# A two-layer decode step on one core: the ninth half rows of the second up projection move to the upper partitions and to GpSimd's queue

## The chip, the core and the metric

The kernel runs on one core of a Trainium2 chip. A core has TensorE (PE), VectorE (DVE), ScalarE (ACT), GpSimd (POOL) and SyncE (SP), an on-chip memory of 128 partitions, and 16 DMA engines that bring data from HBM. Each compute engine follows its own instruction list in order; SP's list holds almost nothing but transfers. The metric is the device time of one execution in microseconds (us), as the median of several.

## The reference

Two layers, each a cached attention and a gated MLP, for two sequences and one new token each; the same weights and the same caches serve both layers. All data are float32.

```python
def attn(x, k_cache, v_cache, wq, wo):      # x: [2, 1, 576]; caches: [2, 32, 8192, 128]
    q = (x @ wq).reshape(2, 1, 32, 128).transpose(0, 2, 1, 3)
    p = softmax(einsum("bhqd,bhkd->bhqk", q, k_cache) * 128 ** -0.5)
    o = einsum("bhqk,bhkd->bhqd", p, v_cache)
    return o.transpose(0, 2, 1, 3).reshape(2, 1, 4096) @ wo
def mlp(x, w_gate, w_up, w_down):           # 576 -> 4608 -> 576
    return (gelu(x @ w_gate) * (x @ w_up)) @ w_down

for _ in range(2):
    x = x + attn(layernorm(x), ...)
    x = x + mlp(layernorm(x), ...)
```

## The kernel before, in words

All large data go through one tile, `space` (L133), of 50176 floats in each of the 128 partitions. A small planner, `Arena` (L68), places every transfer in it. The transfers are written down in one order by `plan_first`, `plan_mlp(0)`, `plan_second` and `plan_mlp(1)` (L324 to L418), and `pump` (L148) issues them from SP in that order as soon as the next one has a place. A place is given back by `done` (L152), after the instructions that read it. `fit` (L107) places the weights of the second layer: first just behind the last one placed, then from the start of `space`, then behind each live region, whichever is clear.

Attention works through 34 items, each two heads (or one) of one sequence. DVE multiplies keys by the query (L644), POOL folds the products (L661), DVE sums them (L664), ACT takes the exponentials (L721), and PE multiplies by the values (L762). In the second layer the items come in reverse. Then `project` (L807) multiplies by eight groups of output weights (L812), in the order 7 to 0, and `add_to_x` (L520) adds the result to x.

`mlp(1)` is where the change lies. `norm` (L486) writes the centred x, transposed, into `xt`: in the window of 32 columns that belongs to u = 0..8, partition p holds the element of x that goes with weight row (9p + u) / 2, in the first or in the second pair of columns by whether 9p + u is even or odd. Its last step is POOL's power (L517). The weights lie in half rows: a row of `w_up` (4608 floats) is cut into two, and of the 1152 half rows partition p holds those with numbers 9p to 9p + 8 (`half_rows`, L221). The gate weights come in three transfers of three half rows per partition. The up weights come in two of three (u = 0..2 and 3..5) and three of one (u = 6, 7, 8), by `GU` (L305). A half row has 2304 floats, 9 KB.

`all_products` (L959) takes them in this order: for each u, two column halves v and four column groups c, a product at L967 of an 8-column window of `xt` with 288 weight columns, added up in `acc`. `activate` (L973) then forms gelu(gate) times up, on ACT and DVE, for the two column halves. Last come the down weights, in eight transfers (`DOWN[1]`, L311) of 9, 9, 5, 4, 3, 3, 2 and 1 rows of 576 floats per partition, and their products at L1004. Between the down products stand a few products without a result (`idle_products`, L524). `add_to_x` and two small output transfers (L1019) end the kernel.

POOL has no work between L517 and the end, and issues no transfer anywhere in the kernel. ACT issues eight small loads of x at the start (L140), two rows each, and one of the two output transfers.

Of the kernel before, what the change touches and what calls it, by code (L numbers as in the profile page):

```python
# [9 lines left out]
F32 = mybir.dt.float32  # L10
# [5 lines left out]
P = 128  # L16
B = 2
# [8 lines left out]
HALF = P // 2  # L26

GH = 4
NU = 9
EQ = 512  # L30
HG = DF // 16
PAD = 6
# [90 lines left out]
def decode_layers(ctx, tc, x_in, kc, vc, wq, wo, wg, wu, wd, out):  # L123
    nc = tc.nc
    scale = DH ** -0.5

    consts = ctx.enter_context(tc.tile_pool(name="consts", bufs=1))
# [15 lines left out]


    arena = Arena()
    queue, ready, places = [], {}, {}

    def pump():  # L148
        while queue and queue[0]():
            queue.pop(0)  # L150

    def done(key):  # L152
        arena.free(key)
        pump()

    def part_at(at, n):
        return space[:, at:at + n]
# [51 lines left out]
    def weights(key, n, first, transfers):  # L209

        def make():
            at = arena.ring(key, n) if first is None else arena.fit(key, n, first)
            if at is None:
                return False
            t = ready[key] = part_at(at, n)
            transfers(t)
            return True

        queue.append(make)

    def half_rows(key, w, us, first):  # L221

        width = w.shape[1] // 2
        rows = w.rearrange("r (s w) -> (r s) w", w=width).rearrange("(p u) w -> p u w", p=P)

        def transfers(t):
            nc.sync.dma_start(t.rearrange("p (u w) -> p u w", w=width), rows[:, us[0]:us[-1] + 1, :])

        weights(key, len(us) * width, first, transfers)

    def of_half(h, k):

        width = wq.shape[1] // 2
        rows = wq.rearrange("r (s w) -> (r s) w", w=width).rearrange("(p u) w -> p u w", p=P)

        def transfers(t):
            for e in range(2):
                nc.sync.dma_start(t[e::2, :], rows[e::2, 2 * k + (h + e) % 2, :])

        weights(("wq", 1, h, k), width, None, transfers)  # L240

    def split_rows(name, w, h, u):

        rows = w[:, DF // 2 * h:DF // 2 * (h + 1)].rearrange("(m r) w -> m r w", r=NU)

        def transfers(t):
            for e in range(2):
                nc.sync.dma_start(t[e::2, :], rows[:, 5 * e + u, :])

        weights((name, 0, h, u), DF // 2, None, transfers)  # L250

    def split_middle(h):

        def transfers(t):
            for g, w in enumerate((wg, wu)):
                for e in range(2):
                    lo, n = DF // 4 * (2 * h + e), DF // 4
                    nc.sync.dma_start(
                        t[e::2, n * g:n * (g + 1)], w[:, lo:lo + n].rearrange("(m r) w -> m r w", r=NU)[:, 4, :]
                    )  # L260

        weights(("gu", 0, h), DF // 2, None, transfers)
# [136 lines left out]
    def plan_mlp(layer):  # L399
        if layer == 0:  # L400
            for h in range(2):
                for u in range(4):
                    split_rows("g", wg, h, u)
                split_middle(h)
                for u in range(4):
                    split_rows("u", wu, h, u)
        else:
            for g, (name, w) in enumerate((("g", wg), ("u", wu))):
                for us in GU[g]:
                    half_rows((name, layer, us[0]), w, us, 0)  # L410
        for rows in DOWN[layer]:
            down(layer, rows)

    plan_first()
    plan_mlp(0)
    plan_second()
    plan_mlp(1)
    pump()  # L418


    ident = consts.tile([P, P], F32, name="ident")
# [37 lines left out]

    xt = consts.tile([P, PAD + NU * 32], F32, name="xt")
    nc.vector.memset(xt, 0.0)


    acc = psum1.tile([P, 2, 512], F32, name="acc")
# [13 lines left out]
    def small(p, n):  # L480

        smalls.append(smalls.pop(0))
        return smalls[0][0:p, 0:n]
# [36 lines left out]
    def add_to_x():  # L520
        nc.vector.tensor_add(x, xps, x)  # L521
# [409 lines left out]
    def mlp(layer):  # L931
        split = layer == 0
        rstd = norm(split)
        if split:
            idle_products(3)
        hT = once.tile([P, 2, NI, 2, 2, B], F32, name="hT", tag="xc")

        def window(u, at):

            return xt[:, PAD + 32 * u - at:PAD + 32 * u - at + 4 * B]  # L940

        def split_products(h):

            steps = [(("g", layer, h, u), u, 2, (0,)) for u in range(4)] + [(("gu", layer, h), 4, 1, (0, 1))]
            steps += [(("u", layer, h, u), u, 2, (1,)) for u in range(4)]
            for key, u, sides, gs in steps:
                w = ready.pop(key).rearrange("p (k c w) -> p k c w", c=4, w=HG)
                for k in range(2):
                    g, e = (k, 0) if u == 4 else (gs[0], k)
                    for c in range(4):  # L950
                        nc.tensor.matmul(
                            acc[32 * c:32 * c + 4 * B, h, :HG], window(u, 4 * g + 2 * e), w[:, k, c, :],
                            start=(key == steps[0][0] and k == 0), stop=(key == steps[-1][0] and k == 1),
                        )
                done(key)
                if key != steps[-1][0]:
                    idle_products(1)

        def all_products():  # L959

            for g, name in enumerate("gu"):
                for us in GU[g]:
                    w = ready.pop((name, layer, us[0])).rearrange("p (u v c w) -> p u v c w", v=2, c=4, w=HG)
                    for u in us:
                        for v in range(2):
                            for c in range(4):
                                nc.tensor.matmul(  # L967
                                    acc[32 * c:32 * c + 4 * B, v, :HG], window(u, 4 * g), w[:, u - us[0], v, c, :],
                                    start=(g == 0 and u == 0), stop=(g == 1 and u == NU - 1),
                                )  # L970
                    done((name, layer, us[0]))

        def activate(v):  # L973

            o = once.tile([P, 2, HG], F32, name="o", tag="row")
            nc.scalar.activation(o[:, 0, :], acc[:, v, :HG], AF.Copy, scale=rstd)  # L976
            gu = o[:, 1, :].rearrange("p (i r) -> p i r", i=NI)
            nc.vector.transpose(gu, o[:, 0, :].rearrange("p (m i) -> p i m", i=NI))  # L978
            g = gu[:, :, 0:4]
            a = once.tile([P, NI, 4], F32, name="ga", tag="part")  # L980
            nc.vector.tensor_mul(a, g, g)
            nc.vector.tensor_scalar(a, a, 0.044715, 1.0, op0=ALU.mult, op1=ALU.add)
            nc.vector.tensor_mul(a, a, g)
            nc.scalar.activation(a, a, AF.Tanh, scale=math.sqrt(2.0 / math.pi))
            nc.vector.scalar_tensor_tensor(a, a, 1.0, g, op0=ALU.add, op1=ALU.mult)
            nc.vector.tensor_mul(a, a, gu[:, :, 4:8])
            a, to = a.rearrange("p i (e b) -> p (i e) b", b=B), hT[:, v].rearrange("p i e s b -> p (i e) s b")
            nc.vector.tensor_scalar_mul(to[:, :, 0, :], a, 0.5)
            nc.scalar.mul(to[:, :, 1, :], a, 0.5)

        if not split:
            all_products()
        for v in range(2):
            if split:
                split_products(v)
            activate(v)
        for n, rows in enumerate(DOWN[layer]):
            if n < len(IDLE[layer]):
                idle_products(IDLE[layer][n])
            w = ready.pop(("d", layer, rows[0])).rearrange("p (i c) -> p i c", c=D)  # L1000
            for k, (t, i) in enumerate(rows):
                v, e = divmod(t, 2) if split else (t % 2, t // 2)
                for c in range(4):
                    nc.tensor.matmul(  # L1004
                        xps[32 * c:32 * c + 2 * B, :], hT[:, v, i, e, :, :].rearrange("p s b -> p (s b)"),
                        w[:, k, c * CW:(c + 1) * CW],
                        start=(rows is DOWN[layer][0] and k == 0), stop=(t, i) == (NT - 1, NI - 1),
                    )
            done(("d", layer, rows[0]))
        add_to_x()  # L1010
        if layer == 0:
            idle_products(1)

    attention(0)
    mlp(0)
    attention(1)
    mlp(1)
# [29 lines left out]
```

## Time and profile before

| | |
|---|---|
| median of 3 runs | 2686.62 us (2686.51 to 2686.68) |
| profiled execution, first to last instruction (its span) | 2685.0 us |
| DMA queue q1 (SP), share of 16 engines' span | 99.8%, 1153.19 MB |
| DVE, POOL, PE busy | 67%, 43%, 34% |
| ACT busy | 6% |
| mean DMA rate | 430 GB/s |

The profiled execution has no other time of its own than its span; the runs' times include some 1.6 us around it. The page gives busy times per engine, the span in 40 slices with the share of the 16 DMA engines that was in use, and the chain of work that ended last. In a group's row stand line, engine, operation, what it writes and reads, count, busy time in us and mean in ns, and after a bar the idle time ahead of it with what ended most of it. In a timeline row the start and the duration come first, in us from the start of the span. In a row of time windows stand the window, its length, busy time and count for PE, weight loads, DVE, ACT and POOL, and then the granted PE clock, the share of the DMA engines in use, and GB/s. No view numbers the DMA engines.

### The profile page before, as it was taken

How to read it: one execution, taken by the hardware profiler on the slowest of the kernel's cores; microseconds unless marked ns; L12 is line 12 of the kernel's file. 1: busy time of each engine (PE TensorE's matmuls, PEld its weight loads, DVE VectorE, ACT ScalarE, POOL GpSimd, SP SyncE). 2: the span in 40 equal slices, each digit the busy share in tenths (PEclk: the TensorE clock that was granted, in tenths of full speed). 3: DMA queues.
4: the chain of work that ended last, by engine and by line, in shares of the span. 5: the costliest groups of instructions: out<-in, count | busy, mean ns of one | idle time of the engine just before them, and what ended most of it. 6: DMA issues, size and time to landing. Idle time of an engine off the chain costs nothing. (4 is left out here: it accounts for less than half of the span.)

```text
span 2685.0 us, 17174 instructions
## 1 busy us (share of the span) xinstructions
PE 914.4 (34%) x7150; PEld 305.4 (11%) x7150; DVE 1806.0 (67%) x874; ACT 163.7 (6%) x786; POOL 1161.8 (43%) x261
## 2 busy tenths in 40 slices
PE   1323332332233233334663333233223323332356
PEld 0100010010001000111221101001000100010022
DVE  4876687677667766867037877667766776776640
ACT  0000000000000000000026000000000000000000
POOL 2543454354445444544028455445444543454420
PEclk7656666665666566566986665666566656656678
DMA  9999999999999999999999999999999999999998
GB/s 422 436 436 426 437 432 434 433 434 432 433 431 435 436 428 433 436 428 425 414 418 434 431 431 436 431 434 434 437 428 434 434 435 431 431 434 435 433 421 375
DMA packets 33950, 1154.30 MB, mean 430 GB/s; under 512 B 4152, under 2 KB 4176, under 8 KB 5968
## 3 DMA queue, kind: packets, MB, share of 16 engines
q1 hardware_dynamic: 33832, 1153.19, 99.8%
q8 instruction: 56, 0.92, 0.1%
q14 instruction: 22, 0.18, 0.0%
q10 hardware_dynamic: 40, 0.01, 0.0%
HBM read 1153.18 MB, written 0.00 MB: 429 GB/s over the span
## 5 line engine op out<-in xcount | busy, mean ns | idle before, releaser
L661 POOL TENSOR_TENSOR space<-space 128x3072 f32<-128x3072 f32 (+3 forms) x221 | 1128.6, 5107 | 1263.3 <-DVE space L644 1202.5
L644 DVE TENSOR_TENSOR space<-space,bank 128x6144 f32<-128x6144 f32 (+3 forms) x223 | 1112.7, 4991 | 560.2 <-DMA space<-in_A_k_cache_dram 496.8
L762 PE MATMUL acc<-space,prz 128*8 128x512 f32 x4096 | 594.6, 744 | 199.4 <-DMA space<-in_A_v_cache_dram 195.5
L664 DVE TENSOR_REDUCE S<-space 128x48 f32<-128x3072 f32 (+3 forms) x223 | 569.3, 2553 | 89.9 <-POOL space L661 89.6
L592 PE MATMUL bank<-qsb,pick 4*64 4x128 f32 (+1 forms) x256 | 46.3, 436 | 863.1 <-DVE space L644 853.1
L762 PEld LDWEIGHTS acc<-space,prz 128*8 128x8 f32 x4096 | 119.1, 104 | 616.3 <-issue 410.6
L784 PE MATMUL bank<-of,osb 128*32 128x2 f32 x512 | 40.9, 202 | 324.4 <-DVE osb L777 324.4
L713 ACT ACTIVATE nbs<-bank 128x2 f32<-128x2 f32 (+1 forms) x68 | 11.6, 171 | 1848.2 <-PE bank L698 1801.8
L592 PEld LDWEIGHTS bank<-qsb,pick 4*64 4x64 f32 (+1 forms) x256 | 20.7, 202 | 882.5 <-DVE space L644 863.2
L517 POOL TENSOR_TENSOR rstd<-ve,mhalf 128x1 f32<-128x1 f32 x4 | 2.2, 550 | 168.8 <-DVE ve L515 168.8
L690 PE MATMUL bank<-ident,m 128*1 128x128 f32 x68 | 19.5, 286 | 160.7 <-DVE m L688 160.5
L784 PEld LDWEIGHTS bank<-of,osb 128*32 128x32 f32 x512 | 35.9, 154 | 331.7 <-DVE osb L777 330.5
L978 DVE STREAM_TRANSPOSE o<-o 128x288 f32<-128x288 f32 x4 | 2.8, 691 | 94.5 <-ACT o L976 94.5
L729 PE MATMUL bank<-sums,unit 128*128 128x2 f32 x120 | 35.2, 363 | 87.0 <-ACT prz L721 87.0
L776 DVE TENSOR_TENSOR acc<-acc,diag 128x512 f32<-128x512 f32 x64 | 43.5, 680 | 22.0 <-PE acc L762 22.0
L721 ACT ACTIVATE prz<-S,nbs 64x128 f32<-64x128 f32 (+1 forms) x128 | 50.7, 396 | 17.3 <-POOL prz L711 14.4
L803 ACT ACTIVATE oT<-bank,rinv 32x8 f32<-32x8 f32 x110 | 28.5, 259 | 381.5 <-PE bank L784 380.8
L654 ACT ACTIVATE space<-space 128x128 f32<-128x128 f32 x164 | 48.3, 296 | 23.6 <-DVE space L644 21.7
L698 PE MATMUL bank<-m,unit 1*128 1x2 f32 (+1 forms) x136 | 39.0, 354 | 25.3 <-DVE m L696 25.3
L777 DVE TENSOR_REDUCE osb<-acc 128x128 f32<-128x512 f32 x64 | 44.3, 691 | 2.2
L521 DVE TENSOR_TENSOR x<-bank,x 128x144 f32<-128x144 f32 x4 | 1.2, 308 | 64.1 <-PE bank L1004 40.4
L729 PEld LDWEIGHTS bank<-sums,unit 128*128 128x128 f32 x120 | 30.1, 311 | 92.2 <-ACT prz L721 92.2
(73 smaller groups left out, 427.6 us busy)
## 6 DMA issues: line engine op xcount, KB each, us to landing
space<-in_A_v_cache_dram SPq DMA_DIRECT2D x8, 4096.0 KB
space<-in_A_k_cache_dram SPq DMA_DIRECT2D x6, 4096.0 KB
space<-in_A_wo_dram SPq DMA_DIRECT2D x15, 1152.0 KB
space<-in_A_k_cache_dram SPq DMA_DIRECT2D x15, 1024.0 KB
space<-in_B_w_down_dram SPq DMA_DIRECT2D x9, 1152.0 KB
space<-in_B_w_gate_dram SPq DMA_DIRECT2D x3, 3456.0 KB
space<-in_A_v_cache_dram SPq DMA_DIRECT2D x10, 1024.0 KB
space<-in_A_wq_dram SPq DMA_DIRECT2D x3, 3072.0 KB
```

Source lines behind the costliest of these rows:

```text
L592: nc.tensor.matmul(qb[n][to, :], pick[32 * c:32 * c + 4, r:r + 1].to_broadcast([4, P // it.heads]), qsb[32 * c:32 * c + 4, (h % 4) * DH:(h ...
L644: nc.vector.tensor_tensor(out=u[:, :rows, :], in0=t[:, :rows, :], in1=qb[n].unsqueeze(1).to_broadcast([P, rows, DH]), op=ALU.mult)
L654: nc.scalar.activation(u[:, j, :], u[:, j, :], AF.Copy, accum_out=S[n][:, k * JC + j:k * JC + j + 1])
L661: nc.gpsimd.tensor_tensor(out=half, in0=half, in1=u[:, :r, DH // 2:], op=ALU.add)
L664: nc.vector.tensor_reduce(out=S[n][:, k * JC:k * JC + own_rows(n, k, m)], in_=prod.pop((n, k)), axis=AX.X, op=ALU.add)
L698: nc.tensor.matmul(mT[n][:, :heads], ones[0:1, :], m1[:, :heads], start=True, stop=True)
L721: nc.scalar.activation(pr[at, lo:].rearrange("p (g e) -> p g e", e=4)[:, 0:it.rows // 2:2, :], s[at, :it.rows].rearrange("p (g r) -> p g r ...
L729: nc.tensor.matmul(tot[n][:, :ITEMS[n].heads], ones, rs.pop(n), start=True, stop=True)
L762: nc.tensor.matmul(accumulator(n)[32 * c:32 * c + 8, :], pr[:, at:at + 8], t[g // 4][:, g % 4 * 4:g % 4 * 4 + 4, :].rearrange("p j d -> p ...
L776: nc.vector.tensor_tensor(out=q, in0=q, in1=diag.unsqueeze(2).to_broadcast([P, 4, DH]), op=ALU.mult)
L777: nc.vector.tensor_reduce(out=t, in_=q.rearrange("p r d -> p d r"), axis=AX.X, op=ALU.add)
L784: nc.tensor.matmul(po[lo:lo + 32, i, :], t[:, i::GH], of, start=True, stop=True)
```

## The change

The half rows with u = 8 of the second layer's up weights, 128 of them, no longer lie one in each partition. They lie in the upper 64 partitions alone, two in each: those of partitions 0 to 63 (s = 0) and of 64 to 127 (s = 1). Each half row is cut into its two column halves (v), and the place, 4608 columns wide, holds v = 0 of s = 0, v = 0 of s = 1, then v = 1 of both; so a half row lies in two pieces of 1152 floats that are apart. The lower 64 partitions of that place hold no weights.

The upper partitions are counted as 32a + 4j + i, with a = 0..1, j = 0..7 and i = 0..3. SP loads the rows with i = 3: two transfers of 16 rows, 144 KB each, ahead of all other up weights. GpSimd loads the rest in twelve transfers, one for each s, i and a, of eight rows (j) in two pieces, 72 KB each. Ahead of each goes a tiny one: eight times two pieces of two floats of x into the unused partitions 0 to 7. GpSimd issues all 24 after the norm of the second MLP (`load_upper`).

The x that belongs to s = 0 must reach the upper partitions: PE copies four columns of the last window from partitions 0 to 63 through the identity, and ACT writes them 32 columns further on into `xt`, which is four columns wider. The products (`upper_products`) are 16 as before, in the same place of the order, each over 64 rows instead of 128.

```diff
-    queue, ready, places = [], {}, {}
+    queue, ready, places, upper = [], {}, {}, []
...
+    def upper_rows(key, w, u):
+
+        width = w.shape[1] // 2
+        rows = w.rearrange("r (s w) -> (r s) w", w=width)
+        rows = rows.rearrange("(s a j i u) (v w) -> s i u a j v w", s=2, a=2, j=8, u=NU, v=2)
+
+        def transfers(t):
+            to = t[HALF:].rearrange("(a j i) (v s w) -> s i a j v w", a=2, j=8, s=2, v=2)
+            upper.append(t[:8].rearrange("p (n v w) -> n p v w", n=12, v=2))
+            upper.extend((to[s, i, a], rows[s, i, u, a]) for s in range(2) for i in range(3) for a in range(2))
+            for s in range(2):
+                nc.sync.dma_start(
+                    t[HALF + 3::4, :].rearrange("p (v s w) -> s p v w", s=2, v=2)[s],
+                    rows[s, 3, u].rearrange("a j v w -> (a j) v w"),
+                )
+
+        weights(key, 2 * width, 0, transfers)
...
             for g, (name, w) in enumerate((("g", wg), ("u", wu))):
+                if name == "u":
+                    upper_rows((name, layer, NU - 1), w, NU - 1)
                 for us in GU[g]:
-                    half_rows((name, layer, us[0]), w, us, 0)
+                    if name == "g" or us[0] < NU - 1:
+                        half_rows((name, layer, us[0]), w, us, 0)
...
-    xt = consts.tile([P, PAD + NU * 32], F32, name="xt")
+    xt = consts.tile([P, PAD + NU * 32 + 2 * B], F32, name="xt")
...
+        def load_upper():
+
+            first = small(P, 2 * B)[HALF:]
+            at = PAD + 32 * (NU - 1)
+            nc.tensor.matmul(first, ident[:HALF, :HALF], xt[:HALF, at:at + 2 * B], start=True, stop=True)
+            nc.scalar.copy(xt[HALF:, at + 32:at + 32 + 2 * B], first)
+            little = x_in[:, 0, :].rearrange("b (j v w) -> (b j) v w", j=4, v=2)[:, :, :2]
+            for n, (to, rows) in enumerate(upper[1:]):
+                nc.gpsimd.dma_start(upper[0][n, :, :, :2], little)
+                nc.gpsimd.dma_start(to, rows)
+
+        def upper_products():
+
+            key = ("u", layer, NU - 1)
+            w = ready.pop(key)[HALF:].rearrange("p (v s c w) -> p s v c w", s=2, v=2, c=4)
+            for s in range(2):
+                for v in range(2):
+                    for c in range(4):
+                        nc.tensor.matmul(
+                            acc[32 * c:32 * c + 4 * B, v, :HG],
+                            xt[HALF:, PAD + 32 * (NU - s) - 4:PAD + 32 * (NU - s) + 4], w[:, s, v, c, :],
+                            start=False, stop=(s == 1),
+                        )
+            done(key)
...
             for g, name in enumerate("gu"):
                 for us in GU[g]:
+                    if name == "u" and us[0] == NU - 1:
+                        upper_products()
+                        continue
...
         if not split:
+            load_upper()
             all_products()
```

## The prediction

> **What bounds the kernel now.** I read the page first: busy shares, DMA slices, queues, the chain that ended last.
>
> ```profile
> span 2685.0 us, 17174 instructions
> ...
> DMA  9999999999999999999999999999999999999998
> ...
> q1 hardware_dynamic: 33832, 1153.19, 99.8%
> ...
> DMA 28%; DVE 13%; POOL 3%; PE 0%; issue 0%; ACT 0%; POOLq 0%; SPq 0%
> ...
> L713 ACT ACTIVATE nbs<-bank 128x2 f32<-128x2 f32 (+1 forms) x68 | 11.6, 171 | 1848.2 <-PE bank L698 1801.8
> ...
> L690 PE MATMUL bank<-ident,m 128*1 128x128 f32 x68 | 19.5, 286 | 160.7 <-DVE m L688 160.5
> ```
>
> The reader sees SP's queue q1 filling 99.8% of the 16 DMA engines for the whole span: the time is 1153 MB at the engines' rate, plus a short head and tail. No other engine is near its limit. The last two rows serve as prices below. The sum is made against the 2685.0 us span; the median of the three runs, 2686.62, is 1.6 us above it, and I carry those 1.6 us over.
>
> Next, the chain after 2600 us in order of time, and the DMA share in stretches of the tail (last two columns: share of the 16 engines, GB/s).
>
> ```profile
> 2603.68 49.37 DMA space<-in_B_w_up_dram
> ...
> 2653.07 27.34 DMA space<-in_B_w_down_dram
> 2680.41 0.04 issue
> 2680.45 0.67 PE bank L1004 x16
> ...
> 2681.66 0.31 DVE x L521
> ```
>
> ```profile
> 2668.00:2672.00 4.00, 3.54 (x88) 2.54 (x92) 0.00 (x0) 0.00 (x0) 0.00 (x0) 1.00 1.00 418
> 2672.00:2674.00 2.00, 1.94 (x40) 1.03 (x32) 0.00 (x0) 0.00 (x0) 0.00 (x0) 1.00 0.99 400
> 2674.00:2676.00 2.00, 1.13 (x33) 0.93 (x34) 0.00 (x0) 0.00 (x0) 0.00 (x0) 1.00 0.73 302
> 2676.00:2678.00 2.00, 1.36 (x30) 0.54 (x24) 0.00 (x0) 0.00 (x0) 0.00 (x0) 1.00 0.53 218
> 2678.00:2679.00 1.00, 0.00 (x0) 0.00 (x0) 0.00 (x0) 0.00 (x0) 0.00 (x0) 1.00 0.55 212
> 2679.00:2680.00 1.00, 0.92 (x24) 0.54 (x24) 0.00 (x0) 0.00 (x0) 0.00 (x0) 1.00 0.43 173
> 2680.00:2681.00 1.00, 0.55 (x16) 0.33 (x16) 0.00 (x0) 0.00 (x0) 0.00 (x0) 1.00 0.07 25
> ```
>
> The stream does not stop at once. The share falls to about 0.53 by 2676-2678 and stays there until 2679: about eight engines have finished while eight still work. The engines get equal shares of every large transfer, so eight run behind the others. Idle engine time from 2672 to 2681 is 0.02 + 0.54 + 0.94 + 0.45 + 0.57 + 0.93 = 3.45 us; less the 0.6 us after the last landing at 2680.41 it is 2.85 us. That is all that any shift of bytes between engines can win: 2683.8 at best. After that landing the end is fixed: last products, the addition, the output.
>
> **The change, part by part.** The rows around it, in order of time (start, duration, engine), with the transfer sizes:
>
> ```profile
> 2579.98 8.84 PE L762 MATMUL acc<-space,prz 128*8 128x512 f32 x61
> ...
> 2590.88 3.10 PE L812 MATMUL bank<-space,oT 128*4 128x144 f32 x93
> ...
> 2595.24 11.56 SPq L227 DMA_DIRECT2D space<-in_B_w_up_dram  x5
> ...
> 2600.89 2.10 PE L812 MATMUL bank<-space,oT 128*4 128x144 f32 x32 [0.68 <-DMA space<-in_A_wo_dram]
> ...
> 2610.57 0.69 DVE L511 STREAM_TRANSPOSE xt<-xc 128x288 f32<-128x288 f32 x1
> ...
> 2611.38 0.55 POOL L517 TENSOR_TENSOR rstd<-ve,mhalf 128x1 f32<-128x1 f32 x1 [38.01 <-DVE ve L515]
> ...
> 2614.77 4.56 PE L967 MATMUL acc<-space,xt 128*8 128x288 f32 x48 [5.19 <-DMA space<-in_B_w_gate_dram]
> ...
> 2647.54 6.73 PE L967 MATMUL acc<-space,xt 128*8 128x288 f32 x80 [2.31 <-DMA space<-in_B_w_up_dram]
> ...
> 2655.88 1.16 PE L967 MATMUL acc<-space,xt 128*8 128x288 f32 x16 [1.62 <-DMA space<-in_B_w_up_dram]
> ...
> 2662.14 4.04 PE L1004 MATMUL bank<-space,hT 128*4 128x144 f32 x72 [3.40 <-DMA space<-in_B_w_down_dram]
> ...
> 2671.69 1.41 PE L1004 MATMUL bank<-space,hT 128*4 128x144 f32 x40
> ```
>
> ```profile
> space<-in_B_w_up_dram SPq DMA_DIRECT2D x2, 3456.0 KB
> ...
> space<-in_B_w_up_dram SPq DMA_DIRECT2D x3, 1152.0 KB
> ```
>
> ```profile
> L1004 PE MATMUL bank<-space,hT 128*4 128x144 f32 x288 | 11.9, 317 | 7.1 <-DMA space<-in_B_w_down_dram 7.0
> ```
>
> *Bytes per engine.* 434 GB/s over 16 engines is 27.1 GB/s each. Removed: one 1152 KB transfer, 72 KB (73.7 thousand bytes) or 2.72 us on each engine. Added on SP: two transfers of 16 rows, 144 KB each, 18 KB or 0.68 us on each engine. Added on GpSimd: twelve transfers of 8 rows of 9 KB, 864 KB together. If a transfer of 8 rows uses eight engines and always the same eight, they take 108 KB or 4.08 us each, the other eight nothing. Net: +2.04 us on the eight, -2.04 us on the others. The total stays the same.
>
> That few rows use few engines is read from the start of the run, where ACT's ring loads x in eight transfers of two rows beside SP's first weights:
>
> ```profile
> 0.74 6.96 SPq L227 DMA_DIRECT2D space<-in_A_wq_dram  x3
> ...
> 1.04 9.65 ACTq L140 DMA_DIRECT2D x<-in_A_x_dram  x8
> ...
> 17.58 0.31 DVE L488 BATCH_NORM_STATS2 stats<-x 128x6 f32<-128x144 f32 x1 [12.61 <-DMA space<-in_A_wq_dram]
> ```
>
> ```profile
> q10 hardware_dynamic: 32, 0.01, 0.2%
> ...
> space<-in_A_wq_dram SPq DMA_DIRECT2D x3, 3072.0 KB
> ```
>
> The second fence is the DMA view of the first 20 us. ACT's ring q10 moved 32 packets for eight transfers: four each, two rows and two end marks, so two engines each. They took 0.2% of 16 x 20 us = 0.64 us, 0.02 us a packet.
>
> [...]
>
> *The tiny ones.* Twelve, each two pieces of 8 bytes and a mark per engine: 36 packets x 0.02 = 0.7 us on their eight engines, and if the large ones' marks go elsewhere too, little more. So -1.3 us on the eight without the large transfers, about +2.3 us on the eight with them.
>
> *When the large ones land.* GpSimd is free at 2611.9, after L517, with nothing behind its 24 issues in this layer, and only the ninth products wait for them. Issuing: the nearest rows are ACT's eight issues in 9.65 us, 1.2 us each, queueing included. That gives 29 us, so 2641; a GpSimd issue appears nowhere, and I bound it by 0.3 us (almost free) and 2.5 us (twice ACT's). Moving: the last x transfer has landed by 17.58, so 16 packets per engine took at most 16.5 us, one per SP packet of 24 KB (24.6 thousand bytes / 27.1 GB/s = 0.91 us): rings take turns packet by packet. A large transfer puts two pieces of 4.5 KB and a mark on an engine: 36 turns. SP's rows are 27 KB (1.02 us) up to the second three-row up transfer, whose products start at 2647.5, then 9 KB (0.34 us). 36 x 1.02 + 24 x 0.17 = 41 us, so 2654 from 2613, without the quicker late turns. That is just before 2655.88, when the ninth products start now. The cover is thin.
>
> What a delay costs: PE waited 7.0 us for down weights, 3.4 of that ahead of the first product; the other 3.6 us is slack. Ninth products up to 2659.5 cost nothing against today's end. The point from which GpSimd decides is therefore (2659.5 - 2611.9)/24 = 2.0 us a transfer.
>
> *Order on SP's queue.* The two 16-row transfers move ahead of the up weights; the 4608-column place is free once the last item's values have been read (L762, done by 2588.9). The placing rule then moves the second three-row up transfer behind output groups 4, 3 and 2 rather than 7, 6, 5: by L812's rows at 2603.0 instead of 2594.0. SP issues the up weights at 2595.2-2606.8 and the engines read 1.03 at 2604-2612:
>
> ```profile
> 2604.00:2612.00 8.00, 3.80 (x66) 2.01 (x56) 2.42 (x8) 0.00 (x0) 0.55 (x1) 0.71 1.03 440
> 2612.00:2640.00 28.00, 13.29 (x152) 4.56 (x156) 0.00 (x0) 0.00 (x0) 0.00 (x0) 0.74 1.00 428
> ```
>
> Three gate transfers of 3456 KB, 8.2 us each, are queued ahead of it. Cost 0; without that cover, up to 9 us.
>
> *Copying x to the upper partitions.* One 64-row product (286 ns at L690) and one ACT copy (171 ns at L713), between the transpose's end at 2611.26 and the first gate products at 2614.77, which wait for weights: 0; uncovered, 0.5 us. The ninth products stay 16, over 64 rows: 0. Four more columns of xt: 0.
>
> *Sum.* If the large ones meet the eight that finish early: they end 2.3 us later, near 2677-2679, and the late eight 1.3 us earlier. The last landing goes from 2680.4 to 2679.1, the span to 2683.7, the median to 2685.3. If they meet the late eight: +2.3 us, 2688.9.
>
> **The rivals.** A is the forecast, 2685.3.
>
> B: the large ones meet the late eight, or late engines lie in both halves: 2.3 us are added to the engine that ends last, 2688.9. For it: no view says which eight are late. [...]
>
> C, the other side by more than the limit: GpSimd's issuing becomes the bound. At 2.5 us a transfer the last is issued at 2611.9 + 60 = 2671.9, 12.4 us past the 2659.5 that costs nothing: 2699. It decides from 2.0 us up, and exceeds 0.2% from 2.2 us. For it: no GpSimd issue was ever timed here, and the turns alone already use 41 of the 47.6 us. Against it: ACT's 1.2 us.
>
> D: the change doesn't do what it says: the eight engines differ from transfer to transfer and the bytes spread evenly: 2686.6 plus up to 0.5 us for the tiny ones.
>
> E: turns are taken by whole shares of a transfer. An engine's share of a three-row transfer is 216 KB, 8.2 us; twelve large ones behind twelve SP transfers would last until the third down transfer, whose products start at 2671.7: 12.2 us past 2659.5, 2698.8. Against it, the x loads: 16 turns behind 192 KB shares would be 116 us, and they took at most 16.5. [...] For GpSimd's ring nothing here shows it.
>
> **How the numbers follow.** A 0.42, B 0.28, C 0.15, D 0.10, E 0.05. The prediction is A, 2685.3. A, B and D all lie within 0.2% (5.4 us, about what a measurement of this kernel can tell from no change), and the 2.85 us bound keeps any rebalancing there: same 0.78. C and E are slower: 0.20. Faster needs a gain that no row shows: 0.02. The range goes from the full balance with 0.4 us to spare, 2683.4, past B to a mild form of C, 2692; A alone is 2683.4 to 2686.6.
>
> **What would show it.** Right: the share in the last 6 us stays near 1 and then drops at once, instead of resting at 0.53; the last landing is near 2679; a ring of GpSimd's carries 864 KB; the ninth products start no later than about 2656; and the up weights leave no gap below 0.95 at 2612-2657. B shows as a longer plateau, D as an unchanged one. C and E show as ninth products that wait past 2659 for the up weights and a PE that then runs down products without waiting. The prediction is wrong if GpSimd's first issue comes late, if one issue costs over 2 us, or if a GpSimd ring costs the engines time that moves no bytes.

## The result

The changed kernel takes 2691.36 us in the median (2690.84 to 2693.15, 20 runs) beside 2686.69 us for the kernel before (2686.38 to 2687.77, 20 runs): 1.0017 times the time, 95% interval 1.0011 to 1.0024. It is slower by 4.7 us, inside the range that was given and within 0.2%, but a gain had been forecast (2685.3). The profiled execution's span is 2689.2 us, 4.2 us longer than before.

From the page of the changed kernel: span, DMA slices, queues and the chain that ended last.

```profile
span 2689.2 us, 17250 instructions
...
DMA  9999999999999999999999999999999999999998
...
q1 hardware_dynamic: 33784, 1152.31, 99.6%
...
q0 software_dynamic: 960, 0.89, 0.1%
...
DMA 28%; DVE 13%; POOL 3%; PE 0%; issue 0%; ACT 0%; POOLq 0%; SPq 0%
```

The bytes went where the change sends them: q0, GpSimd's ring (its own queue on the DMA engines), carries 864 KB and SP's queue that much less. The bound is the same, the stream. Now the stretches of the tail and the end of the chain, with the columns known from the prediction.

```profile
2604.00:2612.00 8.00, 4.78 (x66) 2.52 (x66) 2.17 (x7) 0.00 (x0) 0.00 (x0) 0.50 1.03 442
2612.00:2640.00 28.00, 14.35 (x146) 4.92 (x146) 0.24 (x2) 0.16 (x1) 10.23 (x18) 0.72 1.00 395
2640.00:2657.00 17.00, 8.58 (x80) 2.75 (x84) 0.00 (x0) 0.00 (x0) 3.92 (x7) 0.64 1.00 415
...
2674.00:2676.00 2.00, 2.00 (x48) 1.23 (x36) 0.00 (x0) 0.00 (x0) 0.00 (x0) 1.00 0.86 357
2676.00:2678.00 2.00, 1.88 (x44) 1.32 (x44) 0.00 (x0) 0.00 (x0) 0.00 (x0) 1.00 0.73 288
2678.00:2680.00 2.00, 1.52 (x36) 0.88 (x35) 0.00 (x0) 0.00 (x0) 0.00 (x0) 1.00 0.51 210
2680.00:2682.00 2.00, 1.48 (x34) 0.59 (x25) 0.00 (x0) 0.00 (x0) 0.00 (x0) 1.00 0.41 168
2682.00:2684.00 2.00, 0.84 (x24) 0.54 (x24) 0.00 (x0) 0.00 (x0) 0.00 (x0) 1.00 0.37 143
2684.00:2686.00 2.00, 1.18 (x28) 0.43 (x24) 0.24 (x1) 0.00 (x0) 0.00 (x0) 1.00 0.11 40
```

```profile
2656.72 27.78 DMA space<-in_B_w_down_dram
2684.51 0.04 issue
...
2685.76 0.31 DVE x L542
```

One stretch of the kernel before, for comparison:

```profile
2640.00:2657.00 17.00, 13.08 (x141) 4.39 (x134) 0.00 (x0) 0.00 (x0) 0.00 (x0) 0.75 1.01 425
```

The last landing moves from 2680.41 to 2684.51, by 4.1 us. Three rows carry it:

- 2612 to 2640: the share is 1.00 as before, but the rate is 395 GB/s where it was 428. The engines are busy and move less. (428 - 395) x 28 / 434 = 2.1 us.
- 2640 to 2657: 415 instead of 425 GB/s, 0.4 us.
- The tail is longer. Idle engine time from 2674 to the last landing is 0.28 + 0.54 + 0.98 + 1.18 + 1.26 + 0.29 = 4.5 us (the last is 0.51 less the 0.22 of the last row); before it was 2.83. That is 1.7 us. The share rests at 0.41 and 0.37, that of about six engines, where it rested at about 0.5, that of eight.

Together 4.2 us. From 2657 to 2674 the changed kernel moves a little more than the one before (424 and 420 GB/s, where it was 417 and 412), 0.3 us the other way, so the sum holds to some tenths.

The trace also keeps a record for each packet, that is for each row or piece that an engine moves and for each mark; no view prints them one by one. They place the slow stretch: of SP's 640 rows of 27 KB in the gate and up weights, 79 took over 1.1 us, where 1.03 is usual (3 took that long in the kernel before), and 76 of these start between 2620 and 2635, beside the pieces of the two SP transfers of 16 rows, which start between 2624.5 and 2634.7.

GpSimd's issues in the timeline (the bracket is the idle time ahead and what ended it), and the ninth products:

```profile
2613.02 0.74 POOL L988 DMA_DIRECT2D space<-in_A_x_dram  x1 [0.15 <-POOL rstd L538]
2613.76 0.57 POOL L989 DMA_DIRECT2D space<-in_B_w_up_dram  x1
...
2617.11 0.56 POOL L989 DMA_DIRECT2D space<-in_B_w_up_dram  x1
...
2621.28 0.56 POOL L988 DMA_DIRECT2D space<-in_A_x_dram  x1 [3.61 <-DMA space<-in_A_x_dram]
...
2654.36 0.56 POOL L989 DMA_DIRECT2D space<-in_B_w_up_dram  x1 [0.48 <-DMA space<-in_B_w_up_dram]
...
2663.73 1.15 PE L998 MATMUL acc<-space,xt 64*8 64x288 f32 x16 [1.25 <-DMA space<-in_B_w_up_dram]
```

```profile
L1054 PE MATMUL bank<-space,hT 128*4 128x144 f32 x288 | 10.6, 293 | 3.3 <-DMA space<-in_B_w_down_dram 3.1
...
L989 POOL DMA_DIRECT2D space<-in_B_w_up_dram x12 | 6.7, 560 | 15.3 <-DMA space<-in_B_w_up_dram 15.3
```

An issue takes 0.56 us. The first eight follow each other; from the ninth on GpSimd waits for an earlier landing. So the last issue stands at 2654.36 although issuing itself is cheap, and the ninth products end their wait at 2663.73, 7.9 us later than before. Still PE waits 3.1 us for down weights behind them: the late products do not set the end.

One statement made ahead of the prediction and again in it is wrong: the ninth products are 16 now, but they were eight (two v, four c). A product leaves two records (288 for the 144 products at L967 of the kernel before), so L998 has 32 where the kernel before has the 16 of its row at 2655.88. That is some 1.1 us more of PE, and it is covered in the same way.

### The profile page after: what moved, and what is told of

It is laid out like the page before. It is cut to its first block, busy times and chain, and to the rows that moved or that the text cites. A ratio compares the mean times of both kernels' runs of the same rounds, so it can differ in the third digit from the quotient of the medians.

```text
span 2689.2 us, 17250 instructions
## 1 busy us (share of the span) xinstructions
PE 914.3 (34%) x7168; PEld 304.6 (11%) x7168; DVE 1806.1 (67%) x874; ACT 163.9 (6%) x787; POOL 1175.4 (44%) x285
```

## The experiments

My first theory after the result was that bytes which one half of the engines loses and the other gains make some late engine later (case B of the prediction; the expectations call it placing theory). The rivals were that GpSimd's ring itself costs time (ring theory), that the late ninth products set the end, and that the order on SP's queue does. The first four runs missed both theories, and a second part came from them: a transfer of few rows into one half of the partitions makes packets longer (395 GB/s in the changed kernel and 329 in `pool16`, where the kernel before moved 428), unless the engines that carry it are those that otherwise write to that half. The last clause is the author's supposition: no view numbers the engines. Each kernel was timed beside the kernel before, on the same chip; the medians of that kernel were 2686.5 to 2686.7 us throughout.

### Which part costs: SP or GpSimd, tiny or large

`sp16`: all half rows go to the upper partitions by SP, eight transfers of 16 rows; GpSimd loads nothing.

```diff
-                nc.sync.dma_start(
-                    t[HALF + 3::4, :].rearrange("p (v s w) -> s p v w", s=2, v=2)[s],
...
+                for i in range(4):
+                    nc.sync.dma_start(
+                        t[HALF + i::4, :].rearrange("p (v s w) -> s p v w", s=2, v=2)[s],
+                        rows[s, i, u].rearrange("a j v w -> (a j) v w"),
+                    )
...
-                nc.gpsimd.dma_start(upper[0][n, :, :, :2], little)
-                nc.gpsimd.dma_start(to, rows)
```

> The new layout, copy of x and products stay; SP loads all 128 half rows in eight transfers of 16 rows, GpSimd loads nothing, so every engine gets the same bytes as before. Ring theory (the 24 GpSimd transfers cost all engines time) and placing theory (108 KB on eight engines that include late ones): both expect the time of before, 2686.7 within 0.5 us. Rival, that the layout or SP's changed order costs the time: 2691.

`sp16_tiny`: the same, and GpSimd issues the twelve tiny transfers alone (`nc.gpsimd.dma_start(to, rows)` removed, the other line kept).

> As the kernel with eight SP transfers of 16 rows, and the twelve tiny GpSimd transfers alone, without a large one. Ring theory: half of the 24 transfers' cost remains, +1 to +2.3 us over before, 2687.7 to 2689. Placing theory: the tiny ones hold 1.5 KB, so 2686.7.

`sp8`: the changed kernel's twelve transfers of 8 rows, issued by SP ahead of the two of 16 rows, and no tiny ones.

```diff
-            upper.extend((to[s, i, a], rows[s, i, u, a]) for s in range(2) for i in range(3) for a in range(2))
+            for s in range(2):
+                for i in range(3):
+                    for a in range(2):
+                        nc.sync.dma_start(to[s, i, a], rows[s, i, u, a])
```

> The twelve transfers of eight rows are issued by SP, without tiny ones; GpSimd loads nothing. Placing theory: the 108 KB still fall on eight engines; if late ones are among them, +2.0 us and more, 2689 to 2691; if these eight are all early, about 2685. Ring theory: no GpSimd ring, so nothing beyond the shift of bytes, at most 2688.7.

`pool16`: GpSimd loads its 864 KB in six transfers of 16 rows, without tiny ones.

```diff
+            whole = t[HALF:].rearrange("(q i) (v s w) -> s i q v w", i=4, s=2, v=2)
+            upper.extend((whole[s, i], rows[s, i, u].rearrange("a j v w -> (a j) v w")) for s in range(2) for i in range(3))
...
-                nc.gpsimd.dma_start(upper[0][n, :, :, :2], little)
```

> GpSimd loads its 864 KB in six transfers of 16 rows, without tiny ones: one row on each of 16 engines, bytes spread evenly. Ring theory: a quarter of the transfers, +0.5 to +1.2 us over before, 2687.2 to 2687.9. Placing theory: no shift of bytes, 2686.7. If neither, and a GpSimd ring costs by bytes, 2691.

Measured: `sp16` 2694.02 us, ratio 1.0028 (1.0018 to 1.0039); `sp16_tiny` 2694.27, 1.0029 (1.0018 to 1.0039); `sp8` 2698.33, 1.0042 (1.0028 to 1.0055); `pool16` 2693.3, 1.0024 (1.0015 to 1.0033). The same stretch of time in `sp16`, `sp8` and `pool16`, where the kernel before moved 428 GB/s, and SP's issues in `sp16`:

```profile
2612.00:2640.00 28.00, 14.30 (x130) 4.83 (x134) 0.18 (x2) 0.16 (x1) 0.55 (x1) 0.62 0.88 288
```

```profile
2612.00:2640.00 28.00, 13.93 (x128) 4.38 (x132) 0.00 (x0) 0.16 (x1) 0.20 (x1) 0.62 0.72 256
```

```profile
2612.00:2640.00 28.00, 11.29 (x112) 3.66 (x116) 0.00 (x0) 0.00 (x0) 2.54 (x6) 0.62 1.00 329
```

```profile
2595.42 41.54 SPq L241 DMA_DIRECT2D space<-in_B_w_up_dram  x8
2637.17 2.32 SPq L227 DMA_DIRECT2D space<-in_B_w_up_dram  x4
```

All four are above every time that was expected of them. The ring's tiny transfers are not what costs: twelve of them add 0.25 us to `sp16`, less than can be measured (`all_pool_early` below has the large ones). Two other things do. In `pool16` the engines are busy (1.00) at 329 GB/s: (428 - 329) x 28 / 434 = 6.4 us of the 6.7 us that it loses. In `sp16` and `sp8` the share falls as well, to 0.88 and 0.72: in `sp16` SP's eight issues last 41.54 us, until 2637, and only then come the large transfers behind them. The changed kernel has two such SP transfers, not eight, and its share does not fall; so the order on SP's queue cost it nothing that shows, and would have with more of them.

### A tiny transfer ahead of a large one, or behind it

`tiny_behind`: each tiny transfer follows its large one instead of going ahead.

```diff
-                nc.gpsimd.dma_start(upper[0][n, :, :, :2], little)
                 nc.gpsimd.dma_start(to, rows)
+                nc.gpsimd.dma_start(upper[0][n, :, :, :2], little)
```

> The changed kernel with each tiny transfer behind its large one. [...] Placing theory alone (which eight get the bytes): 2688 to 2691. If the order of tiny and large doesn't matter: 2691.4.

Measured: 2698.55 us, 1.0044 (1.003 to 1.0057).

```profile
2620.00:2630.00 10.00, 5.48 (x48) 1.70 (x48) 0.00 (x0) 0.00 (x0) 1.89 (x4) 0.66 1.02 323
2630.00:2640.00 10.00, 3.69 (x40) 1.29 (x44) 0.00 (x0) 0.00 (x0) 2.58 (x5) 0.66 0.98 295
```

This is more than either time that was expected. The bytes and the pieces are the same as in the changed kernel, and the engines move 323 and 295 GB/s at a share of about 1. In the packet records 341 of SP's 640 rows of 27 KB now take over 1.1 us, where 79 did, and they begin at the first large transfer, not beside SP's 16-row ones. The order of the pair decides this, and it costs 7 us (2698.55 beside 2691.36). That swapping the pair moves the large ones to the other eight engines is the author's estimate: the 7 us fit it, but no view numbers the engines.

### Half the partitions, or every second one

`two_halves` and `two_parities` start from the kernel before. The ninth half rows stay where they were, on all 128 partitions, and SP loads them in two transfers of 64 rows: in the one kernel the lower and the upper half, in the other the even and the odd partitions.

```diff
+            if key == ("u", 1, NU - 1):
+                for h in range(2):
+                    nc.sync.dma_start(t[HALF * h:HALF * (h + 1), :], rows[HALF * h:HALF * (h + 1), NU - 1, :])
+                return
```

> The kernel before, with one edit: the ninth half rows, still one in each partition, come in two SP transfers, lower 64 partitions and upper 64, instead of one of 128. No GpSimd, no new layout. [...] Rival (the cost lies with the layout's reads or GpSimd): 2686.7.

> [...] Rival (two transfers of 64 rows cost more than one of 128, whatever the partitions): the same as by halves.

Measured: `two_halves` 2695.45 us, 1.0032 (1.0019 to 1.0044); `two_parities` 2686.62, 1.0000 (0.9991 to 1.0009). First `two_halves`, then `two_parities`, then the kernel before:

```profile
2640.00:2650.00 10.00, 7.65 (x76) 2.50 (x72) 0.00 (x0) 0.00 (x0) 0.00 (x0) 0.67 1.00 357
2650.00:2660.00 10.00, 4.59 (x56) 1.19 (x44) 0.00 (x0) 0.00 (x0) 0.00 (x0) 0.84 1.05 240
```

```profile
2650.00:2660.00 10.00, 7.07 (x88) 2.37 (x77) 1.78 (x7) 0.85 (x3) 0.00 (x0) 0.97 1.03 438
```

```profile
2650.00:2660.00 10.00, 7.13 (x80) 2.48 (x72) 1.84 (x7) 0.91 (x4) 0.00 (x0) 0.90 1.02 436
```

Two transfers instead of one cost nothing. It is where they write that costs: into one half, 240 GB/s with the engines at 1.05, where the kernel before moved 436. The size is more than that rate explains: 1152 KB at 240 GB/s, a mean over 10 us with other transfers in it, would take 4.9 us, 2.2 us more than at 434, and the median is 8.9 us longer. The packet records of the profiled run (2694.02 us) show where the rest lies: the two halves have 128 rows of 9 KB, but 247 rows of that size took over 0.4 us (3 in the kernel before), and the 256 rows of 20736 bytes of the down transfers behind them took 0.95 us in the mean instead of 0.78. So other transfers' rows stretch too; why as much as they do stays open.

### Do the late ninth products matter

`after_early`: the changed kernel with its 24 GpSimd issues moved forward, behind attention's last products with the values. `all_pool`: the changed kernel with all 16 groups of eight rows loaded by GpSimd, and 16 tiny ones; SP loads none of the ninth half rows.

```diff
@@ after_early, in attention
             values(N - 1)
+            load_rows()
             finish(n)
@@ all_pool, in upper_rows
-            upper.extend((to[s, i, a], rows[s, i, u, a]) for s in range(2) for i in range(3) for a in range(2))
-            for s in range(2):
-                nc.sync.dma_start(
...
+            upper.extend((to[s, i, a], rows[s, i, u, a]) for s in range(2) for i in range(4) for a in range(2))
```

> The changed kernel with its 24 GpSimd issues moved ahead, behind the last values' products of the attention, some 27 us earlier; nothing else. [...]

> GpSimd loads all sixteen groups of eight rows, each with a tiny transfer ahead; SP's two transfers of 16 rows are gone. [...] Ring theory (each GpSimd transfer costs all engines): 32 transfers instead of 24, 2692 to 2693.

Measured: `after_early` 2691.12 us, 1.0016 (1.0007 to 1.0025); `all_pool` 2699.04, 1.0047 (1.0034 to 1.006). The ninth products in `after_early` (a group's row) and its stretch 2612 to 2640, then the same stretch and the ninth products in `all_pool`:

```profile
L1002 PE MATMUL acc<-space,xt 64*8 64x288 f32 x32 | 2.1, 403 | 0.0
```

```profile
2612.00:2640.00 28.00, 13.54 (x124) 4.71 (x124) 2.42 (x8) 0.16 (x1) 1.12 (x2) 0.62 1.01 397
```

```profile
2612.00:2640.00 28.00, 15.22 (x144) 4.83 (x144) 0.00 (x0) 0.00 (x0) 9.38 (x17) 0.72 1.00 425
```

```profile
2675.47 2.10 PE L993 MATMUL acc<-space,xt 64*8 64x288 f32 x16 [16.36 <-DMA space<-in_B_w_up_dram]
```

In `after_early` the ninth products wait for nothing, and the time is that of the changed kernel within 0.3 us: their lateness cost the changed kernel nothing. With four groups more it decides: in `all_pool` the second half of them starts at 2675.47, and the loss is 12.5 us, where at most 2693 was expected, although the stretch is not slowed (425 GB/s). And in that kernel, which has no SP transfers of 16 rows, the 395 GB/s of the changed kernel is gone (one row of 27 KB over 1.1 us), while `after_early`, which has them, keeps 397: those two transfers made it, not the twelve large ones.

### Bytes on one half alone

`all_pool_early` is `all_pool` with its issues moved forward as in `after_early`. `lower_early` is its mirror: the rows go to the lower 64 partitions, x of the upper ones is copied down, and the tiny ones follow the large ones, so that, by the same supposition, these meet the other eight engines.

```diff
@@ lower_early
-            to = t[HALF:].rearrange("(a j i) (v s w) -> s i a j v w", a=2, j=8, s=2, v=2)
+            to = t[:HALF].rearrange("(a j i) (v s w) -> s i a j v w", a=2, j=8, s=2, v=2)
...
-            nc.tensor.matmul(first, ident[:HALF, :HALF], xt[:HALF, at:at + 2 * B], start=True, stop=True)
+            nc.tensor.matmul(first, ident[HALF:, HALF:], xt[HALF:, at:at + 2 * B], start=True, stop=True)
```

> All sixteen groups by GpSimd with a tiny transfer ahead of each, issued behind the last values' products. [...] What is left is the byte shift of 2.7 us onto eight engines: if six of the late ones are among them, 2689 to 2690; if the earlier +12.5 us of the same kernel with late issue came from the ring itself: 2697 or more.

> [...] If late engines lie in both halves: +2.7 us again, 2689 to 2690. If all late ones are in the upper half: they lose 2.7 us of work, 2684 to 2685. [...]

Measured: `all_pool_early` 2690.13 us, 1.0013 (1.0004 to 1.0022); `lower_early` 2689.79, 1.0011 (1.0002 to 1.002). First `all_pool_early`, then `lower_early`:

```profile
2620.00:2630.00 10.00, 7.16 (x68) 2.17 (x63) 0.00 (x0) 0.00 (x0) 2.23 (x4) 0.67 1.01 425
...
2678.00:2680.00 2.00, 1.92 (x39) 0.95 (x35) 0.00 (x0) 0.00 (x0) 0.00 (x0) 1.00 0.38 160
2680.00:2682.00 2.00, 0.91 (x24) 0.52 (x24) 0.00 (x0) 0.00 (x0) 0.00 (x0) 1.00 0.39 157
```

```profile
2620.00:2630.00 10.00, 6.37 (x64) 2.00 (x60) 0.00 (x0) 0.00 (x0) 2.23 (x4) 0.67 1.00 421
...
2678.00:2680.00 2.00, 1.51 (x38) 0.87 (x34) 0.00 (x0) 0.00 (x0) 0.00 (x0) 1.00 0.31 127
2680.00:2682.00 2.00, 0.84 (x24) 0.46 (x24) 0.00 (x0) 0.00 (x0) 0.00 (x0) 1.00 0.15 58
```

Hardly anything is slowed here, and both directions lose: 3.5 and 3.1 us. 1152 KB on eight engines is 5.44 us each, less the 2.72 us of the transfer that goes: +2.7, and with the prediction's 0.26 us for marks, taken 16/12 times, +3.1. The plateaus count the engines that are last: 0.39 x 16 is six in `all_pool_early`, 0.15 x 16 is two in `lower_early`. If the two kernels load opposite eights, which no view shows, six of the eight late engines lie among those that the first one loads and two among the others, and no shift by halves can help both. What makes eight engines late is not shown by any row.

### Even bytes, by GpSimd, without slowed packets

`native_early`: the old layout; GpSimd loads the ninth half rows early, in 16 transfers of eight rows, lower and upper half in turn. That successive transfers of eight rows meet alternating eights, and so the same half of the partitions each time, was the author's estimate.

```diff
+            to = t.rearrange("(s a j i) w -> s i a j w", s=2, a=2, j=8)
+            upper.extend((to[s, i, a], rows[s, i, u, a]) for i in range(4) for a in range(2) for s in range(2))
```

> The old layout, one ninth half row in each of 128 partitions, loaded by GpSimd early in sixteen transfers of eight rows that alternate between lower and upper partitions; no tiny ones, no copy of x. [...]

It took 2693.05 us, 1.0023 (1.0014 to 1.0032), a loss of 6.4 us. Two more kernels ask why. `upper_first` swaps the halves (`for s in (1, 0)`). `two_pieces` puts the two column halves of each half row 4.5 KB apart, so that a row is two pieces as in the changed kernel.

```diff
-            to = t.rearrange("(s a j i) w -> s i a j w", s=2, a=2, j=8)
+            to = t.rearrange("(s a j i) (v h w) -> s i a j v h w", s=2, a=2, j=8, v=2, h=2)[:, :, :, :, :, 0, :]
```

> The sixteen early transfers of GpSimd as before them (eight rows each, lower and upper half in turn, no tiny ones), but each half row goes into two places of 4.5 KB that are apart, as in the changed kernel; the place is 4608 columns wide. Theory P: with two pieces a row the eight engines alternate between the halves, as the changed kernel's pairs of a tiny and a large one showed, and it was the single piece of 9 KB that broke this in the run before: no stretch (420 GB/s or more in 2590-2610), bytes spread evenly, 2686.6 to 2687.0. Rival Q: engines do not alternate for transfers that follow each other without a tiny one between, whatever the pieces: the same 355 to 365 GB/s in 2590-2610 and about 2693.

> The sixteen early transfers in single pieces of 9 KB, the upper half first in each pair. [...] If the engines do not alternate (or drift) with single pieces, order changes little: about 2693, with 355 to 365 GB/s in 2590-2610. If the order of the halves had been the wrong one in the run before: no stretch and 2686.6.

Measured: `upper_first` 2692.97 us, 1.0023 (1.0014 to 1.0032); `two_pieces` 2687.21, 1.0002 (0.9993 to 1.0011). The kernel before, `native_early`, `upper_first` and `two_pieces`:

```profile
2590.00:2600.00 10.00, 6.66 (x168) 4.83 (x168) 0.64 (x3) 0.00 (x0) 0.00 (x0) 0.87 1.02 423
2600.00:2610.00 10.00, 6.44 (x102) 3.27 (x98) 1.16 (x5) 0.00 (x0) 0.00 (x0) 0.62 1.04 440
```

```profile
2590.00:2600.00 10.00, 6.44 (x136) 4.80 (x136) 1.40 (x4) 0.00 (x0) 5.08 (x10) 0.83 1.03 363
2600.00:2610.00 10.00, 3.26 (x64) 1.75 (x64) 0.00 (x0) 0.00 (x0) 1.04 (x2) 0.61 1.04 354
```

```profile
2590.00:2600.00 10.00, 6.26 (x136) 4.84 (x136) 1.34 (x4) 0.00 (x0) 5.02 (x10) 0.83 1.02 348
```

```profile
2590.00:2600.00 10.00, 5.62 (x152) 4.37 (x156) 0.54 (x3) 0.00 (x0) 4.55 (x9) 0.89 1.02 418
...
2678.00:2680.00 2.00, 0.92 (x24) 0.54 (x24) 0.00 (x0) 0.00 (x0) 0.00 (x0) 1.00 0.49 193
2680.00:2682.00 2.00, 1.10 (x24) 0.43 (x24) 0.31 (x1) 0.00 (x0) 0.00 (x0) 1.00 0.05 18
```

With two pieces a row the transfers behave as if they alternate: nothing is slowed, the tail is that of the kernel before, and the time cannot be told from it. (Its place in `space` is also twice as wide; no run separates that.) With one piece a row the order of the halves changes nothing, so these transfers seem not to alternate. If all of them met the same eight engines, half of them would, by the same supposition, write to the half that these do not otherwise write to, and these eight would get 2.7 us of bytes more: (423 - 363 + 440 - 354) x 10 / 434 = 3.4 us, and 2.7, make 6.1; measured were 6.4. That is an estimate; the packet records agree with it as far as packets can be joined end to start: in `native_early` GpSimd's rows mostly follow each other on one engine after one or two SP rows, in `two_pieces` there are mostly four or five SP rows between one pair and the next. Which engines these are is not shown, since no view numbers them, nor why one piece or two should decide it.

## Why the prediction was wrong

**What bounds the kernel** held. The stream sets the end, and `after_early` shows that the late ninth products do not. No kernel of this study is faster than the one before, as the bound of 2.85 us allows little.

**The choice of A failed.** The sum for bytes stands: 2.0 us and 0.3 us for marks, gained or lost; with 2.7 us for the bytes, 3.1 in all, `lower_early` measures 3.1 and `all_pool_early` 3.5. But the step "if the large ones meet the eight that finish early" took the late engines for one half. By the plateaus they are six in one and two in the other, the second clause of case B, and the changed kernel's large ones meet the six: by B's sum 2688.9. That the large ones always meet the same eight engines, and the tiny ones the other eight, on which the +2.3 and -1.3 us rest, no run shows; `all_pool_early` and `lower_early` show the 3.5 and 3.1 us just named, and `tiny_behind` shows that the order of the pair decides 7 us. The choice of A over B was the author's estimate. Extra packets of x and the output could not have settled it: x has 32 packets of 0.02 us, 0.64 us in all, and the late engines end some 4 to 5 us behind the others.

**A term was missing**: the two SP transfers of 16 rows were costed at their bytes, 0.68 us. They slow other transfers' packets by 2.1 us per engine in addition; the row of 2612 to 2640 shows it (395 instead of 428 GB/s), and `all_pool`, without them, has 425. B's 2688.9 and 2.1 us make 2691.0; 2691.36 was measured. That this lies in the range is luck: the upper end was set for a mild form of C, and what came near it was B and a cost that no rival had. The prediction named "a GpSimd ring costs the engines time that moves no bytes" as a danger; the time that moves no bytes was there, but it came with the 16-row transfers of SP, as `all_pool` without them shows; six of GpSimd's own cost it too (`pool16`).

**When the large ones land** was off in both its prices. A GpSimd issue costs 0.56 us, near the lower bound of 0.3; ACT's 1.2 us was too high a measure. The turns gave 2654; eight in flight and some 2 us from landing to landing made it 2663.7. That is 4.2 us past the 2659.5 from which it was to cost something, and it cost nothing: the 3.6 us of slack was counted against the old end, and the end itself moved 4.1 us. C's mechanism shows in `all_pool`, by landings and not by issuing.

**Order on SP's queue and copying x**: cost 0 both. The share is 1.03 at 2604 to 2612 and 1.00 at 2612 to 2657, and `sp16` shows where the cover ends. The copy of x is done at 2612.83, and the first gate products wait for their weights until 2614.92.

**D and E** are false. The bytes do not spread evenly in the changed kernel: its tail rests at 0.41 and 0.37 for 4 us more. For E: with eight in flight, the twelfth large issue at 2654.36 follows the landing of the eighth large one. Eight had landed in the 41 us from 2613, and only five whole shares of 8.2 us fit in there. So the engines do not finish SP's share of a transfer before they turn to GpSimd's ring.

## What to carry to other kernels

Where a kernel is bound by its transfers, look at GB/s beside the share of the engines: a share of 1.00 with a lower rate means that packets take longer (395 GB/s in the changed kernel, with 79 of 640 rows over 1.1 us where 3 were before). Here that came with transfers of few rows into one half of the partitions, and it cost about three times what the bytes of the transfer take (2.1 us for 0.68, 8.9 for 2.7). Spread every transfer over both halves of the partitions (`two_parities`), or find an order of issue in which the rate holds, as in `all_pool_early` and `lower_early` (425 and 421 GB/s); that their few-row transfers meet the engines that otherwise write there is the author's estimate. And before bytes are moved between engines to even out a tail, find out which engines are late: a plateau tells how many there are, not that they form one group.

## What the runs showed that was not expected

- Splitting one transfer into two by halves of the partitions costs 8.9 us, splitting it by even and odd partitions nothing (2695.45 and 2686.62 us).
- A GpSimd transfer costs 0.56 us of issue here, and from the ninth on an issue waits for an earlier landing; twelve tiny ones are nearly free (0.25 us).
- One tiny transfer ahead of a large one or behind it decides 7 us (2691.36 and 2698.55 us), and whether a row is one piece or two decides 6 us (2693.05 and 2687.21 us).
- Eight or more few-row transfers on SP's queue starve the stream behind them: the share of the engines is 0.88 in `sp16` and 0.72 in `sp8` for 28 us.
